# The short split tile of the first layer moves from last place to second place

## The chip, the cores and the metric

The kernel runs on one core of a Trainium2 chip. The metric is device time in microseconds (us) of one launch. The engines are TensorE (PE: matrix products and transposes; PEld: its weight loads), VectorE (DVE), ScalarE (ACT), GpSimd (POOL) and the queue engine SyncE (SP), which issues most of the DMAs. ScalarE issues some DMAs itself.

## The reference, cut to what matters

Three parts follow one another: a linear recurrence ("attention") over 4 sequences of 768 steps with 8 heads of 48, then two feed-forward layers on its 3072 x 384 output.

```python
# attention, for each step t
y[:, :, t] = einsum('bhd,bhde->bhe', rt, state + u[None] * kt (x) vt)
state      = wt[:, :, :, None] * state + kt (x) vt
# first layer, d_ff 2048
h = maximum(x @ w_in, 0);  x2 = (h * h) @ w_out
# second layer, d_ff 1536
out = ((x2 @ w_a) * (x2 @ w_b)) @ w_out2
```

## The kernel before, in words

**Units.** The recurrence is cut into chunks of 128 steps. One sequence's chunk is a *unit*; there are 24, ordered by chunk first, so that units 0 to 3 are chunk 0 of the four sequences, units 4 to 7 chunk 1, and so on. A unit passes through three functions: `prepare` (VectorE scans L197 and L202 and the scaled keys and receptances, GpSimd and ScalarE for the diagonal; it also issues the four loads of the unit after next, `load_unit(i + 2)`), `scores` (TensorE L239 and L243, VectorE L247) and `mix` (TensorE L261, L267 and L274, the new state L292 and L294, and six small SyncE copies, L287). A unit's result is 128 columns of the first layer's input. `split_x` (L306, L307) writes it as a rounded high part and a low rest into the input tile `xt[n]` of the first-layer tile it belongs to.

**First-layer tiles and stages.** The first layer runs over tiles of 2 or 4 units (256 or 512 columns). The list is `tiles`, L187. For each tile a stage of 16 steps runs. In step f, TensorE forms `hp` from `w_in[f]`, ScalarE and VectorE form relu squared (L463, L464), `split_g` splits it (L371, L372), and two steps later `x2_step` adds `w_out[f-2]` times it to three sums `acc`. At the end `store_acc` evicts the sums (L398) and stores them to DRAM. The tile in first place, units 0 and 1, is different: its products are plain fp32 products without a split (L417, L410; each counts as two matmuls in the trace). All others take three matmuls for each product, high by high, high by low and low by high (`mm3`, L311 to L313).

**What runs beside a stage.** While the stage of one tile runs, the units of the *next* tile are computed: `bursts` makes a plan that says after which step's `hp` the `scores` and the `mix` of a unit are issued; `BURSTS = (0, 2, 4, 6, 7, 9, 11, 13)` holds for four units. Before the change stage 0 (units 0 and 1) has units 2 to 5 beside it, stage 1 (units 2 to 5) has 6 to 9, stages 2, 3 and 4 have four units each, stage 5 (units 18 to 21) has the two units 22 and 23, and stage 6 (units 22 and 23, 256 columns) has none.

**Weights.** Weights arrive as 64-bit values. `decode` (L41 to L44, two ScalarE and two VectorE operations) turns one 128 x 384 block into fp32. The 32 blocks of the first layer are decoded in stage 0, two in a step. `split_w1` (L144, L145) splits them for `mm3`, from step 12 of stage 0 on and two in a step of stage 1. The 36 blocks of the second layer are loaded, decoded and stored back to DRAM as fp32 (`narrow_load`, `narrow_store`, called the narrow decodes here) from stage 2 on in the program's order; `load_w2` and `split_w2` (L167, L168) bring them in again during the last stage.

**Order.** Every engine works through its own queue in order. That order is not the program's: a planner, which schedules the instructions against its own estimate of the time, places work ahead where it finds an engine free and a buffer available, and otherwise takes the earlier part of the program first. Weight blocks share 36 buffers (`wp`), the loads of a unit have two (`ld`; `v` three), the input tiles two (`xp`), `A` two.

**Second layer.** Six tiles of 512 columns follow, 12 steps each, with TensorE alone near its limit.

Of the kernel before, what the change touches and what calls it, by code (L numbers as in the profile page):

```python
# [23 lines left out]
NU = len(units)  # L24
# [4 lines left out]
BURSTS = (0, 2, 4, 6, 7, 9, 11, 13)  # L29
# [18 lines left out]
@with_exitstack  # L48
def kernel(
    ctx: ExitStack,  # L50
    tc: tile.TileContext,
    krT: bass.AP,
    wT: bass.AP,
    krn: bass.AP,
    vn: bass.AP,
    u: bass.AP,
    w1: bass.AP,
    w2: bass.AP,
    w3: bass.AP,
    w4: bass.AP,  # L60
    w5: bass.AP,
    out: bass.AP,
):
    flags = ctx.enter_context(tc.tile_pool(name="flags", bufs=1))
    xs = ctx.enter_context(tc.tile_pool(name="xs", bufs=1, space=bass.MemoryType.DRAM)).tile([NT, DM], F32, name="xs")
    flag = chunked_path(tc, flags, krT, wT, krn, vn, u, w1, w2, w3, w4, w5, out)
    with tc.If(tc.nc.values_load(flag, min_val=0, max_val=1) > 0):
        stepwise_path(tc, xs, krT, wT, vn, u, w1, w2, w3, w4, w5, out)
# [3 lines left out]
def chunked_path(ctx, tc, flags, krT, wT, krn, vn, u, w1, w2, w3, w4, w5, out):  # L72
# [111 lines left out]
        loaded[i] = w, kr, v, nn  # L184

    xt = {}
    tiles = [(0, 1)] + [tuple(range(i, i + 4)) for i in range(2, NU - 2, 4)] + [(NU - 2, NU - 1)]  # L187
    x0 = {}
    unit = {}

# [62 lines left out]
    def mix(i):  # L253
# [22 lines left out]
        def post():  # L276
            if i > 1:
                x = at.tile([128, G, C], F32, tag="x", name="xf", bufs=2)
            else:
                if i == 0:  # L280
                    x0[0] = xp.tile([128, G, 2, C], F32, tag="x", name="x0")
                x = x0[0][:, :, i, :]
            for rows in ((slice(0, GP),) if c > 0 else (slice(0, D), slice(64, GP))):
                act.activation(out=x[rows], in_=ps[rows], func=AF.Copy)
            for p0 in (0, 64):
                for m in range(3):
                    sync.dma_start(out=x[p0 + 48:p0 + 64, m], in_=x[p0 + 16 * m:p0 + 16 * m + 16, 3])  # L287
            if c < NC - 1:
                src = pk[0:GP]
                if c > 0:  # L290
                    t = at.tile([GP, G, 2, D], F32, tag="kt", name="t")
                    dve.tensor_tensor(out=t, in0=src, in1=s[:, :, :, 0:D], op=ALU.add)  # L292
                    src = t
                dve.tensor_tensor(  # L294
                    out=s[:, :, :, 0:D], in0=src, in1=st["pe2"].to_broadcast([GP, G, 2, D]), op=ALU.mult
                )
            return (lambda: split_x(i, x)) if i > 1 else None
        return post

    def split_x(i, xf):  # L300
        n, o = (i + 2) // 4, (i + 2) % 4
        if n not in xt:
            xt[n] = xp.tile([128, 2, 3, T], F32R, tag="x", name="x")
        o = slice(o * C, (o + 1) * C)
        hi, lo = xt[n][:, 0, :, o], xt[n][:, 1, :, o]
        act.activation(out=hi, in_=xf[:, 0:3], func=AF.Copy)  # L306
        dve.tensor_tensor(out=lo, in0=xf[:, 0:3], in1=hi.bitcast(F32), op=ALU.subtract)  # L307
# [68 lines left out]
    def bursts(units_of, at_steps):  # L376

        return {f: (units_of[n // 2], n % 2) for n, f in enumerate(at_steps) if n // 2 < len(units_of)}
# [30 lines left out]
        for m in range(3):  # L409
            pe.matmul(out=acc[m], lhsT=w_out[f][:, m * 128:(m + 1) * 128], rhs=t, start=f == 0, stop=f == 15)  # L410

    plan = bursts(tiles[1], BURSTS)
    prepare(2)
    for f in range(16):
        hp = p_mm.tile([128, N], F32, tag="mm", name="hp")
# [6 lines left out]
        t = gg[f] = gp.tile([128, N], F32, tag="gh", name="g")  # L422
# [18 lines left out]
    for n in range(1, len(tiles)):  # L441
# [12 lines left out]
        plan = {} if last else bursts(tiles[n + 1], BURSTS)  # L454
        if not last:
            prepare(tiles[n + 1][0])
        for f in range(16):
# [4 lines left out]
            t = gp.tile([128, N], F32, tag="t", name="t", bufs=2)  # L462
# [265 lines left out]
```

## Time and profile before

| | us |
|---|---|
| median of 3 runs (1028.87 to 1030.48) | 1030.08 |
| profiled execution, its own time | 1029.76 |
| span from its first to its last instruction | 1028.1 |
| TensorE busy in it | 984.1 |
| VectorE busy | 540.5 |
| ScalarE busy | 448.3 |

The profiled execution is one launch; its span leaves 1.7 us outside the program's instructions. TensorE's matmuls overlap in the record (one of 512 columns shows some 0.39 us and the next begins after 0.23), so a busy TensorE is not TensorE at its pace; where pace matters, the starts of matmuls that follow each other are to be read. An edge between stages is taken where ScalarE begins the first eviction of a stage's sums (L398).

### The profile page before, as it was taken

The numbers are of one execution on the slowest core, as the hardware profiler recorded it, in microseconds if no ns is written. First come the engines' busy times: TensorE is split into PE (matmuls) and PEld (weight loads), VectorE is DVE, ScalarE is ACT, GpSimd is POOL, SyncE is SP. The second block draws the span as 40 slices with busy tenths as digits, with TensorE's granted clock in tenths as the row PEclk, the third lists the DMA queues.
The fourth block names the chain that finished last, engine by engine and source line by source line (L and its number), as shares of the span: only waits on it lengthen the run. The fifth ranks groups of instructions, "written<-read, shape, count | busy, mean of one in ns | idle before, by whom it ended". The sixth has DMA issues, their size and how long they took to land. (4 is left out here: it accounts for less than half of the span.)

```text
span 1028.1 us, 13834 instructions
## 1 busy us (share of the span) xinstructions
PE 984.1 (96%) x5250; PEld 834.4 (81%) x5250; DVE 540.5 (53%) x908; ACT 448.3 (44%) x930; POOL 72.7 (7%) x60
## 2 busy tenths in 40 slices
PE   3789999998999999999999999999999999999996
PEld 2577777777788888887889988888888888888885
DVE  8999999988856756644346622222222222222221
ACT  5788676777555444543336612222322312212211
POOL 4234201000100100000000000000000000000000
PEclk9999999999999999999999999999999999999998
DMA  9677237877422221201015400100100100000001
GB/s 274 218 254 244 67 95 254 258 257 244 146 83 64 77 67 54 65 21 54 23 46 155 132 1 2 61 1 21 41 1 1 41 1 16 27 1 32 0 1 34
DMA packets 47020, 88.15 MB, mean 86 GB/s; under 512 B 7008, under 2 KB 25568, under 8 KB 46944
## 3 DMA queue, kind: packets, MB, share of 16 engines
q1 hardware_dynamic: 40464, 77.74, 24.5%
q10 hardware_dynamic: 6480, 9.44, 2.6%
q8 instruction: 43, 0.70, 0.3%
q14 instruction: 33, 0.27, 0.1%
HBM read 69.46 MB, written 16.52 MB: 84 GB/s over the span
## 5 line engine op out<-in xcount | busy, mean ns | idle before, releaser
L536 DVE TENSOR_TENSOR t<-ap,t 128x512 f32<-128x512 f32 x72 | 49.8, 691 | 278.7 <-PE ap L313 278.7
L371 ACT ACTIVATE gh<-t 128x512 fp32r<-128x512 f32 (+1 forms) x168 | 102.4, 609 | 185.3 <-DVE t L536 127.0
L372 DVE TENSOR_TENSOR gl<-t,gh 128x512 fp32r<-128x512 f32 (+1 forms) x168 | 112.1, 667 | 74.7 <-ACT gh L371 74.4
L527 ACT ACTIVATE t<-bp 128x512 f32<-128x512 f32 x72 | 43.1, 598 | 160.4 <-PE bp L313 159.7
L311 PE MATMUL hp<-x,w 128*128 128x512 f32 (+1 forms) x288 | 109.3, 379 | 2.7 <-DVE t L464 2.7
L312 PE MATMUL acc<-gl,w 128*128 128x512 f32 (+1 forms) x288 | 108.2, 376 | 1.9 <-DVE gl L372 1.8
L313 PE MATMUL acc<-gh,w 128*128 128x512 f32 (+1 forms) x288 | 107.5, 374 | 0.0
L312 PE MATMUL hp<-x,w 128*128 128x512 f32 (+1 forms) x288 | 107.2, 372 | 0.0
L313 PE MATMUL hp<-x,w 128*128 128x512 f32 (+1 forms) x288 | 107.1, 372 | 0.0
L311 PE MATMUL acc<-gh,w 128*128 128x512 f32 (+1 forms) x288 | 102.6, 383 | 0.0
L464 DVE TENSOR_TENSOR t<-t,hp 128x512 f32<-128x512 f32 (+1 forms) x96 | 61.0, 635 | 74.0 <-ACT t L463 74.0
L518 PE MATMUL acc<-w,gh 128*128 128x384 f32 x288 | 96.8, 336 | 0.0
L519 PE MATMUL acc<-w,gh 128*128 128x384 f32 x288 | 96.7, 336 | 0.0
L520 PE MATMUL acc<-w,gl 128*128 128x384 f32 x288 | 95.1, 337 | 0.0
L463 ACT ACTIVATE t<-hp 128x512 f32<-128x512 f32 (+1 forms) x96 | 53.3, 555 | 83.2 <-PE hp L313 81.3
L313 PE MATMUL bp<-x,w 128*128 128x512 f32 x216 | 85.3, 395 | 0.0
L312 PE MATMUL bp<-x,w 128*128 128x512 f32 x216 | 85.1, 394 | 0.0
L312 PE MATMUL ap<-x,w 128*128 128x512 f32 x216 | 84.1, 390 | 0.0
L313 PE MATMUL ap<-x,w 128*128 128x512 f32 x216 | 84.1, 389 | 0.0
L311 PE MATMUL ap<-x,w 128*128 128x512 f32 x216 | 84.1, 389 | 0.0
L311 PE MATMUL bp<-x,w 128*128 128x512 f32 x216 | 83.8, 390 | 0.0
L311 PEld LDWEIGHTS hp<-x,w 128*128 128x128 f32 x288 | 54.2, 188 | 14.4 <-DVE t L464 4.3
(93 smaller groups left out, 1713.5 us busy)
## 6 DMA issues: line engine op xcount, KB each, us to landing
raw<-in_w SPq DMA_DIRECT2D x68, 384.0 KB, 4.7
lkr<-in_krT SPq DMA_DIRECT2D x24, 448.0 KB, 4.1
nn<-in_krn SPq DMA_DIRECT2D x24, 384.0 KB, 3.9
w2d<-f SPq DMA_DIRECT2D x36, 192.0 KB, 2.8
ws<-w2d SPq DMA_DIRECT2D x36, 192.0 KB, 2.5
lw<-in_wT SPq DMA_DIRECT2D x24, 226.2 KB, 3.4
vn<-in_vn SPq DMA_DIRECT2D x24, 192.0 KB, 2.8
out<-e ACTq DMA_DIRECT2D x24, 192.0 KB, 1.9
```

The lines of the kernel that those rows point to most:

```text
L311: pe.matmul(out=out, lhsT=wt[:, 0, sl], rhs=rhs_hi, start=first, stop=False)
L312: pe.matmul(out=out, lhsT=wt[:, 0, sl], rhs=rhs_lo, start=False, stop=False)
L313: pe.matmul(out=out, lhsT=wt[:, 1, sl], rhs=rhs_hi, start=False, stop=last)
L371: act.activation(out=gh, in_=t, func=AF.Copy)
L372: dve.tensor_tensor(out=gl, in0=t, in1=gh.bitcast(F32), op=ALU.subtract)
L463: act.activation(out=t, in_=hp, func=AF.Relu)
L464: dve.tensor_tensor(out=t, in0=t, in1=hp, op=ALU.mult)
L518: pe.matmul(out=acc[t], lhsT=ph[:, sl], rhs=w_o[f][:, 0, :], start=(f == 0), stop=False)
L519: pe.matmul(out=acc[t], lhsT=ph[:, sl], rhs=w_o[f][:, 1, :], start=False, stop=False)
L520: pe.matmul(out=acc[t], lhsT=pl[:, sl], rhs=w_o[f][:, 0, :], start=False, stop=(f == 11))
L527: act.activation(out=bs, in_=bp, func=AF.Copy)
L536: dve.tensor_tensor(out=bs, in0=ap, in1=bs, op=ALU.mult)
```

## The change

The first layer's tiles hold 2, 2, 4, 4, 4, 4 and 4 units in place of 2, 4, 4, 4, 4, 4 and 2. The tile in second place now has units 2 and 3, the next ones 4 to 7, 8 to 11, 12 to 15, 16 to 19 and 20 to 23. A table `place` tells `split_x` which tile and which quarter of it a unit has. Stage 0 has two units beside it, with their scores and mixes at steps 1, 5, 8 and 12; stages 1 to 5 have four units each, stage 6 has none and 512 columns.

```diff
     xt = {}
-    tiles = [(0, 1)] + [tuple(range(i, i + 4)) for i in range(2, NU - 2, 4)] + [(NU - 2, NU - 1)]
+    tiles = [(0, 1), (2, 3)] + [tuple(range(i, i + 4)) for i in range(4, NU, 4)]
+    place = {i: (n, o) for n, t in enumerate(tiles) for o, i in enumerate(t)}
     x0 = {}
...
     def split_x(i, xf):
-        n, o = (i + 2) // 4, (i + 2) % 4
+        n, o = place[i]
...
-    plan = bursts(tiles[1], BURSTS)
+    plan = bursts(tiles[1], (1, 5, 8, 12))
     prepare(2)
```

## Rows read from the trace of the kernel before

**Rows 1.** The page, busy time: us, share of the span, instructions of each engine.
```profile
PE 984.1 (96%) x5250; PEld 834.4 (81%) x5250; DVE 540.5 (53%) x908; ACT 448.3 (44%) x930; POOL 72.7 (7%) x60
```

**Rows 2.** Start and length of stage 0's first evictions on ScalarE.
```profile
121.84 0.65 ACT L398 ACTIVATE ev<-acc 128x256 f32<-128x256 f32 x2
```

**Rows 3.** Stages: length, busy of PE, PEld, DVE, ACT, POOL, clock, DMA share, GB/s.
```profile
0.00:43.54 43.54, 21.43 (x111) 17.06 (x111) 38.23 (x62) 25.75 (x61) 17.31 (x24) 1.00 0.76 236
43.54:121.84 78.30, 72.91 (x444) 60.32 (x444) 78.30 (x144) 61.02 (x145) 25.42 (x15) 1.00 0.66 210
121.84:210.63 88.79, 87.57 (x465) 68.72 (x464) 85.41 (x152) 66.29 (x141) 9.43 (x6) 1.00 0.61 194
210.63:298.09 87.46, 81.55 (x459) 64.88 (x458) 70.55 (x120) 54.86 (x120) 10.71 (x8) 1.00 0.58 187
298.09:382.78 84.69, 84.69 (x497) 69.41 (x496) 55.36 (x88) 40.34 (x88) 9.87 (x8) 1.00 0.24 73
382.78:465.21 82.43, 82.43 (x473) 67.14 (x472) 48.42 (x79) 39.48 (x86) 0.00 (x0) 1.00 0.16 48
465.21:536.98 71.77, 71.77 (x371) 59.22 (x370) 27.22 (x42) 24.65 (x44) 0.00 (x0) 1.00 0.12 35
536.98:582.09 45.11, 45.11 (x329) 42.64 (x328) 31.41 (x69) 30.40 (x71) 0.00 (x0) 1.00 0.55 162
```

**Rows 4.** The same stretches, VectorE's first scan of a unit (L197) alone.
```profile
0.00:43.54 43.54, 6.50 (x4) 1.00 0.76 236
43.54:121.84 78.30, 6.08 (x5) 1.00 0.66 210
121.84:210.63 88.79, 5.71 (x4) 1.00 0.61 194
```

**Rows 5.** Stage 1, VectorE's first decode operation (L42) alone.
```profile
121.84:210.63 88.79, 12.36 (x21) 1.00 0.61 194
```

**Rows 6.** Stage 1, VectorE's second decode operation (L44) alone.
```profile
121.84:210.63 88.79, 11.50 (x21) 1.00 0.61 194
```

**Rows 7.** VectorE groups of a step, shapes apart: count, busy us, mean ns, idle before.
```profile
L372 DVE TENSOR_TENSOR gl<-t,gh 128x512 fp32r<-128x512 f32 x152 | 105.3, 693 | 73.7 <-ACT gh L371 73.5
L464 DVE TENSOR_TENSOR t<-t,hp 128x512 f32<-128x512 f32 x80 | 54.3, 679 | 69.6 <-ACT t L463 69.6
L372 DVE TENSOR_TENSOR gl<-t,gh 128x256 fp32r<-128x256 f32 x16 | 6.7, 421 | 0.9 <-ACT gh L371 0.9
L464 DVE TENSOR_TENSOR t<-t,hp 128x256 f32<-128x256 f32 x16 | 6.7, 418 | 4.4 <-ACT t L463 4.4
```

**Rows 8.** First-layer weights on VectorE: ns min/median/max, first and last start us.
```profile
L44 DVE SCALAR_TENSOR_TENSOR wf<-raw,wf x32: 522/544/736, 30.0 to 110.3; 128x384 int32<-128x384 int32 x32
L145 DVE TENSOR_TENSOR w<-wf,w x32: 524/543/1368, 105.7 to 151.6; 128x384 fp32r<-128x384 f32 x32
```

**Rows 9.** TensorE in stages 4 and 6: start, length; nine matmuls between the two.
```profile
430.58 0.39 PE L311 MATMUL hp<-x,w 128*128 128x512 f32 x1
...
432.63 0.39 PE L311 MATMUL acc<-gh,w 128*128 128x512 f32 x1
...
556.59 0.28 PE L311 MATMUL hp<-x,w 128*128 128x256 f32 x1
...
557.67 0.28 PE L311 MATMUL acc<-gh,w 128*128 128x256 f32 x1
```

**Rows 10.** TensorE's parts of a unit: start, length.
```profile
123.16 0.55 PE L243 MATMUL pt<-ident,lkr 112*128 112x112 f32 x4
...
211.33 0.60 PE L261 MATMUL py<-lkr,s 112*112 112x128 f32 x4
211.87 1.08 PE L267 MATMUL py<-A,vn 128*48 128x128 f32 x16
212.88 1.02 PE L274 MATMUL pk<-vn,kt 128*112 128x96 f32 x8
...
436.80 1.16 PE L239 MATMUL ps<-lkr 48*128 48x128 f32 x16
```

## The prediction

> **What bounds the kernel now.** I read the busy times first: TensorE is busy for 96% of the span, VectorE for 53% [rows 1]. These are means over unlike stages, so I cut the span at the first eviction of each stage's sums (stage 0 ends at 121.84 us [rows 2]) and read the busy times stage by stage. The reader is to see two regimes [rows 3]. From 43.54 to 121.84 VectorE is busy for 78.30 of 78.30 us and in stage 1 for 85.41 of 88.79; TensorE's work has to wait for it there. From stage 3 on TensorE is busy all the time and VectorE for 59% and less: stages 3 and 4 (four units beside 512 columns) take 84.69 and 82.43 us, and 82.43 is what such a stage costs when nothing holds it up. Stage 2 lies between: 87.46 us, VectorE at 81%, with narrow decodes left over.
>
> The change alters no matmul. The same products run in the same shapes; a stage of 256 columns goes to the front and one of 512 to the end, and units 4 and 5, 8 and 9, 12 and 13, 16 and 17, 20 and 21 each run one stage later. So TensorE's own work is unchanged, and the time can change only by how long TensorE is held up, which is in the first 300 us. The sum is made by stages; what follows the first layer (from 582.09 us on) is taken as it is.
>
> **The change, part by part.**
>
> *Stages 0 and 1 together, by VectorE.* VectorE works for 38.23 + 78.30 + 85.41 = 201.9 us up to 210.63 us and idles 5.3 (before 43.54) and 3.4 us (stage 1) [rows 3]. Three things leave this stretch. Two units: stage 3 has 55.36 us of VectorE for four units and 16 steps; a step of 512 columns is 0.679 + 0.693 us [rows 7], so 16 are 22.0, and a unit is (55.36 - 22.0)/4 = 8.4 us; two are 16.8. The width: 16 x (0.679 + 0.693 - 0.418 - 0.421) = 8.5 us [rows 7]. The narrow decodes that run there now: 21, with 12.36 + 11.50 = 23.9 us [rows 5, 6], 1.14 us each. That leaves 201.9 - 16.8 - 8.5 - 23.9 = 152.7 us of work and with the old 8.7 us idle an end at 161.4.
>
> Two things correct it. First, work ahead: there are 9 first scans by 121.84 where stage 0 needs 6 (units 0 to 5), and 13 by 210.63 where 10 are needed [rows 4]. Three preparations therefore stand in the 201.9 us that the stretch didn't need. I put a preparation at two thirds of a unit, 5.6 us (an estimate), and take one fewer ahead, as the stretch is shorter: -5.6; the bounds are none fewer (0) and all three (-16.8). Second, some narrow decodes come back: they can't begin before the weight buffers come free, behind the last split at 151.6 [rows 8], which gave 21 in the 59 us up to 210.63; the splits end a little earlier after the change, some 15 us ahead of the new edge, so 5 of them: +5.7 us (bounds 0 and 8). Stage 1 would end at 161.4 - 5.6 + 5.7 = 161.5 us; bounds 152 (below) and 174 (the second rival). TensorE's side allows that: 288 matmuls of 256 columns at 1.08/9 = 0.120 us [rows 9] are 34.6 us. A unit is 0.55 + 2 x 0.60 + 1.08 + 1.02 + 1.16 = 5.0 us by its shown lengths [rows 10]; each carries a tail that the next covers (L267 shows 1.08 and is followed after 1.01), so I take 4.4, with 3.9 and 5.0 as ends. Four units make 17.6, stage 1's own work 52 us.
>
> ScalarE (61.02 of 78.30 and 66.29 of 88.79 us [rows 3]) loses its share of the same two units and of the width, so it stays under VectorE. On SyncE's queue the loads of units 6 and 7 (issued by `prepare` of 4 and 5) and twelve small copies leave stage 0; GpSimd has the two products of each unit with them. Both are far from full (GpSimd 25.42 of 78.30, DMA share 0.66 [rows 3]). I price that at nothing while VectorE sets the pace; if it doesn't, it helps stage 0. No wait is added; what changes is what stands in front of what on VectorE's queue.
>
> *Stages 2 and 3.* Both now have 512 columns and four units, as before. But 31 narrow decodes are left for them instead of 15. Stage 2 lost 87.46 - 82.43 = 5.0 us with 15, or 0.34 each; 31 cost 10.4, and stage 3's own loss of 2.3 stays. Together 2 x 82.43 + 10.4 + 2.3 = 177.5 us against 172.15. Bounds: 169 (decodes as pure filler with 0.1 each) and 190 (first rival's density and beyond). I take 0.34 because it is the only stage with both.
>
> *Stage 4:* 82.4 as before. *Stages 5 and 6:* 71.77 + 45.11 = 116.9 us now, with TensorE busy throughout. They gain two units (8.8) and 288 matmuls that go from 0.120 to (432.63 - 430.58)/9 = 0.228 us each [rows 9], 31.1 us: 156.8. The loads and splits of the second layer's weights that share stage 6 get more room, since VectorE's 31.41 us there grow by 8.5 and the stage by over 25; nothing is late next there. Bounds 155 and 159, by the unit's price and the edges.
>
> *Sum.* 161.5 + 177.5 + 82.4 + 156.8 = 578.2 us against 582.1: 3.9 less. The profiled execution took 1029.76 us (span 1028.1 and 1.7 around it), 0.3 under the median of 1030.08, so 1025.9; I say **1026 us**.
>
> *A rule that speaks against it.* TensorE was granted its full clock, 1.00 (2.4 GHz), in each of these stretches, also up to 43.54 where it is busy for 21.43 us [rows 3]. The Trainium skill, "TensorE: Matmul & The Clock Gate", section "What's actually happening", says that the engine falls back to 1.2 GHz after an idle spell, and the changed stage 1 leaves TensorE idle more often. By the rows the term is zero; by the rule it is the last rival.
>
> **The rivals.**
>
> *1. The decodes jam stage 2 (slower).* If the planner keeps three preparations ahead and the decodes go as early as they can, stage 1 ends at 161.4 + 5.7 = 167.1, and stage 2 has VectorE work of 55.36 + 31 x 1.14 = 90.7 us, more than the 82.4 of TensorE. At stage 1's density (85.41/88.79 = 96%) it takes 94.3. With 84.7, 82.4 and 156.8 the edge is at 585.3, +3.2: **1033**. It decides from a stage 2 over 94 us. For it: stage 2 already suffers with half as many decodes. Against: nothing needs them before the last stage, and the earlier part of the program goes first. At stage 2's own density of 81% it would be 112 us and 1051, the tail.
>
> *2. Stage 0 does not get shorter (slower).* The last of the 32 weight blocks is decoded at 110.3 us [rows 8] and the last steps need it; three preparations ahead say that VectorE had time beyond stage 0's own needs, so the stream of weights may set its end. Then stage 0 ends at 121.8 as now, stage 1 is TensorE's 52 us, ending at 174, decodes run in VectorE's spare time as today, stages 2 and 3 take 172.2: 174 + 172.2 + 82.4 + 156.8 = 585.4, +3.3: **1033**. Against: two units' loads fewer in the queue.
>
> *3. No work ahead (faster).* VectorE needs only 161.4 - 16.8 = 145 us, stage 0 ends near 100, and TensorE's 52 us end stage 1 at 152. With all 36 decodes after it (164.9 + 12.2 + 2.3 = 179.4), 82.4 and 156.8 the edge is at 570.6: **1018**. For it: the units are taken when they are needed. Against: in both edges of today three were ahead.
>
> *4. The clock falls in stage 1 (slower).* TensorE's 52 us at half the clock are 104: some 52 us more, **1078**. The granted 1.00 beside a half-idle TensorE speaks against it.
>
> **How the numbers follow.** Forecast 0.43, its own range 1021 to 1031; rival 1 0.18; rival 2 0.20; rival 3 0.17; rival 4 0.02. About 0.2% (2.1 us, 1028.0 to 1032.1) is what a measurement of this kernel tells from no change. Faster: 0.33 of the forecast and all of rival 3, 0.50. Within: 0.08 of the forecast, 0.05 each of rivals 1 and 2, 0.18. Slower: the rest, 0.32. The range of 1015 to 1037 takes in rivals 1 to 3 with a few us on either side and leaves out the tails.
>
> **What would show it.** In the changed profile: stage 0 ends between 95 and 112 us and stage 1 between 156 and 167, with VectorE busy for 95% and more up to there; fewer than 10 narrow decodes before that edge; stages 2 and 3 together some 177 us; stage 6 at some 74 us with TensorE busy all through; clock 1.00. A stage 0 over 118 is rival 2, a stage 2 over 94 with VectorE above 95% is rival 1, an edge of stage 1 at 152 or earlier rival 3. The prediction is wrong if stages 5 and 6 miss 156.8 by more than 3 us, since there I assumed that only TensorE counts.

## The result, and the profile after

The changed kernel takes 1040.4 us (median of 4 runs, 1039.29 to 1048.03), the kernel before 1029.88 in the same comparison: ratio 1.0122, 95% interval 1.0086 to 1.0158. The forecast was 1026, with a range from 1015 to 1037. The change makes the kernel slower, by 1.2%. The profiled span is 1037.6 us, 9.5 more than before.

First the page of the kernel after: the busy times, as in [rows 1], and the granted clock in 40 slices.

```profile
PE 990.3 (95%) x5250; PEld 842.1 (81%) x5250; DVE 536.7 (52%) x908; ACT 449.0 (43%) x930; POOL 78.0 (8%) x60
PEclk9899998999999999999999999999999999999999
```

The work is the same: 5250 matmuls, 908 VectorE instructions. The stages of the kernel after, cut as in [rows 3] (length, busy time of PE, PEld, DVE, ACT, POOL, clock, DMA share, GB/s); the edges are the first evictions of a stage's sums, and the last row is the second layer.

```profile
0.00:43.60 43.60, 19.68 (x111) 15.49 (x111) 37.05 (x62) 25.90 (x61) 19.13 (x24) 0.96 0.75 235
43.60:120.72 77.12, 70.71 (x411) 58.67 (x412) 77.12 (x143) 58.66 (x136) 22.07 (x13) 0.96 0.65 203
120.72:195.09 74.37, 68.49 (x512) 60.60 (x511) 69.52 (x138) 54.83 (x139) 16.50 (x8) 0.95 0.61 193
195.09:271.28 76.19, 72.74 (x356) 57.86 (x356) 59.68 (x106) 51.81 (x104) 5.02 (x4) 1.00 0.68 217
271.28:354.28 83.00, 83.00 (x482) 68.24 (x482) 56.21 (x90) 40.32 (x89) 9.87 (x8) 1.00 0.26 79
354.28:439.05 84.77, 84.77 (x498) 69.56 (x497) 53.93 (x88) 39.98 (x88) 5.46 (x4) 1.00 0.21 64
439.05:519.08 80.03, 80.03 (x451) 65.10 (x450) 38.25 (x63) 33.70 (x68) 0.00 (x0) 1.00 0.16 47
519.08:587.31 68.23, 68.23 (x302) 56.51 (x301) 38.37 (x66) 36.41 (x69) 0.00 (x0) 1.00 0.37 107
587.31:1037.60 450.29, 442.61 (x2138) 390.05 (x2136) 106.59 (x157) 107.41 (x183) 0.00 (x0) 1.00 0.06 18
```

The reader is to see three things. Stage 0 ends at 120.72, hardly before the old 121.84. Stage 1, with half the columns, still takes 74.37 us, and VectorE is busy for 69.52 of them. And the back as a whole is near the forecast: stages 4 to 6 and what follows them take 1037.6 - 354.28 = 683.3 us, where the forecast had 82.4 + 156.8 + 446.0 = 685.2 (its parts missed by more, see below). So the net error stands in the first 354 us: 354.3 measured, 161.5 + 177.5 = 339.0 forecast, 15.3 too little.

An edge of a stage is not an edge of TensorE's work: its first products of stage 2 start at 186.29 us, 9 us before stage 1 ends. The counts of TensorE instructions in brackets tell where two stages of the same number hold different work.

### The profile page after: what moved, and what is told of

It is laid out like the page before. It is cut to its first block, busy times and chain, and to the rows that moved or that the text cites. A ratio compares the mean times of both kernels' runs of the same rounds, so it can differ in the third digit from the quotient of the medians.

```text
span 1037.6 us, 13812 instructions
## 1 busy us (share of the span) xinstructions
PE 990.3 (95%) x5250; PEld 842.1 (81%) x5250; DVE 536.7 (52%) x908; ACT 449.0 (43%) x930; POOL 78.0 (8%) x60
```

## The experiments

All medians are compared with the kernel before in the same comparison (1029.7 to 1031.9 us there).

**Holding the units back.** Does stage 0 keep its length because units are prepared in it, or because of the stream of weights?

```diff
-    def prepare(i):
+    hold = [None]      # last step of the stage before, for units 4 to 11; then None
+    def prepare(i):
+        if hold[0] is None:
+            return prepare_now(i)
+        with tc.issue_after(hold[0]):
+            prepare_now(i)
...
```

> The changed kernel, all work kept, with VectorE's part of the preparation of units 4 to 7 queued behind the last step of stage 0, and of 8 to 11 behind the last step of stage 1. Theory A: work ahead on VectorE is what kept stage 0 at its old length, so it now ends at 98 to 108 us, and stage 1 ends at 172 to 185 us; 1025 to 1034 us. Theory B: the weights' stream sets the end of stage 0, so it still ends at 116 to 121 us, the units come too late and the kernel takes 1040 to 1055 us.

Measured: 1045.12 us, ratio 1.0154 (1.0126 to 1.0181). Stages 0, 1 and 2 of this kernel:

```profile
0.00:102.56 102.56, 74.11 (x386) 60.41 (x386) 91.65 (x173) 76.53 (x177) 20.38 (x25) 0.96 0.67 212
102.56:169.94 67.38, 61.20 (x478) 55.50 (x479) 60.31 (x116) 44.94 (x109) 10.03 (x8) 0.90 0.69 214
169.94:271.68 101.74, 91.57 (x508) 72.81 (x507) 95.95 (x160) 68.61 (x153) 24.34 (x16) 0.97 0.66 207
```

Stage 0 ends at 102.6, so the weights' stream does not set its end: the preparation of units on VectorE does. But stage 2 ends at 271.68 (271.28 without the hold): what was pushed back is paid there, and the total is no better, against the 1025 to 1034 that theory A expected.

**Without the narrow decodes on VectorE.** The two VectorE operations and one of the two ScalarE operations of each narrow decode are left out, so the second layer works on wrong weights.

```diff
-        sync.dma_start(out=w2d[n], in_=decode(nc, wr.tile(...), raw, near))
+        f = wr.tile([128, 384], F32, tag="ws", name="f")
+        high = raw.rearrange("p (n i) -> p n i", i=2)[:, :, 1]
+        act.activation(out=f, in_=high.bitcast(F32), func=AF.Copy, scale=0.05)
+        sync.dma_start(out=w2d[n], in_=f)
```

> The changed kernel with the 36 narrow decodes cut to one ScalarE copy each (no VectorE operation; the second layer then computes on wrong weights). Theory A, VectorE's queue sets the end of stage 1, because the planner still puts the decodes and the preparations of later units there: the 14 decodes that end before that edge leave it, some 15 us, so stage 1 ends near 180 us in place of 195 and the kernel takes 1022 to 1030 us. Theory C, TensorE's spells at half clock (17 us in the changed kernel's profile) make the loss: the time stays within 4 us of 1040. Theory B, the stream of first-layer weights sets it: stage 0 ends at 121 as before, which A also allows, and stage 1 still ends over 190.

> The kernel before with the same cut of the narrow decodes. Theory A: stages 1 and 2 lose less, stage 1 ends near 205 (210.6 before) and stage 2 takes 83 to 85 us (87.5), 1018 to 1024 us in all. So the changed order, without decodes, would be at most 8 us slower than the old one. Theory C: 1027 to 1031, no change, and the distance to the changed order stays at 10.

Measured: changed order 1030.16 us, ratio 0.9998 (0.9981 to 1.0015); old order 1025.02, 0.9944 (0.9922 to 0.9965). The changed order without them, stages 0 to 2:

```profile
0.00:120.76 120.76, 92.95 (x521) 76.56 (x522) 114.71 (x204) 84.59 (x198) 41.99 (x36) 0.99 0.69 215
120.76:174.53 53.77, 51.65 (x400) 46.39 (x400) 40.80 (x86) 37.82 (x99) 4.21 (x4) 1.00 0.59 198
174.53:260.59 86.06, 83.45 (x453) 66.52 (x452) 56.90 (x87) 49.59 (x108) 9.89 (x8) 1.00 0.73 240
```

Stage 1 falls from 74.37 to 53.77 us and VectorE in it from 69.52 to 40.80. A part of that is work of stage 2 that no longer runs there (TensorE has 400 instructions in place of 512). At the end of stage 2 the gain is 271.28 - 260.59 = 10.7 us. By the medians the decodes cost the changed order 10.2 us and the old one 5.0; 5 us between the orders remain.

**Putting the decodes later.** All of them kept, but none before the end of stage 1 (changed order) or of stage 2 (both orders), at one in 1.6 and 1.3 steps of the program.

```diff
-            elif (n - 2) * 16 + f >= narrow_n[0] * 1.6:
+            elif n > 2 and (n - 3) * 16 + f >= narrow_n[0] * 1.3:
...
+        with tc.issue_after(edge[0]):      # the last gl of stage 2 (or of stage 1, with 1.6)
             sync.dma_start(out=w2d[n], in_=decode(nc, wr.tile(...), raw, near))
```

> The changed kernel, all work kept, with VectorE's part of the narrow decodes queued behind the last step of stage 1 and spread over later steps. Theory A: stage 1 ends near 180 us, stages 2 and 3 pay for 36 decodes in place of 22 with 3 to 6 us, 1029 to 1035 us in all. Theory C: 1037 to 1041.

> The changed kernel, all work kept, with VectorE's part of the narrow decodes queued behind the last step of stage 2. Theory A2, the sum of VectorE's work up to the end of stage 2 sets that edge (271 to 272 us in the changed kernel and in both variants that only shifted work inside this stretch): the edge falls to 258 to 263 us as without the decodes, stages 3 and 4 have room for them at a cost of 0 to 3 us, and the kernel takes 1029 to 1034 us. Rival, the decodes cost TensorE the same wherever they run: 1038 to 1042.

> The kernel before with the same shift of the decodes behind stage 2. Theory A2: its end of stage 2 falls from 298 to 290 to 294 us, 1025 to 1029 us in all, faster than both kernels. Rival, the decodes cost the same wherever they run: 1029 to 1031.

Measured: changed order, behind stage 1, 1040.13 us, 1.0096 (1.0062 to 1.0130); behind stage 2, 1040.3, 1.0101 (1.0080 to 1.0121); old order, behind stage 2, 1035.15, 1.0047 (1.0027 to 1.0067). No gain anywhere, against the expectations. Stages 1 and 2 of the first, stages 2 and 3 of the second, and stage 3 of the third:

```profile
120.88:175.92 55.04, 52.91 (x405) 47.28 (x404) 44.98 (x92) 35.91 (x95) 4.63 (x4) 1.00 0.35 105
175.92:271.71 95.79, 90.67 (x486) 72.13 (x485) 83.75 (x146) 68.16 (x142) 10.77 (x8) 0.96 0.75 245
```

```profile
177.08:258.27 81.19, 81.19 (x450) 66.08 (x449) 55.85 (x90) 38.53 (x83) 9.28 (x8) 1.00 0.24 71
258.27:360.21 101.94, 93.73 (x522) 74.48 (x521) 87.68 (x154) 73.19 (x155) 15.21 (x8) 0.97 0.75 245
```

```profile
289.21:392.63 103.42, 95.03 (x527) 74.89 (x526) 87.08 (x154) 72.78 (x154) 17.89 (x8) 0.97 0.75 242
```

The stages freed of decodes become fast, and the one right behind the gate takes them all: VectorE's instructions in stage 3 rise from 90 to 154, 64 more for some 32 decodes of two each. Stage 3 takes 101.94 and 103.42 us where the kernels after and before need 83.00 and 84.69, although VectorE is busy for 86% and 84% of it only (30 to 40 more instructions of TensorE run in it, so not all of that is lost). So it was not VectorE's sum up to the end of stage 2 alone that mattered, as I had thought by then: the planner issues all decodes at once where it may.

**Spreading the decodes.** Each decode may start only behind the latest step's `gh` and `gl`, so that they come one by one in the program's order; all work is kept, in both orders.

```diff
+        with tc.issue_after(at_step[0]), tc.issue_after(at_step[1]):
             sync.dma_start(out=w2d[n], in_=decode(nc, wr.tile(...), raw, near))
...
+        at_step[:] = [a, d]      # split_g: the ScalarE copy gh and the VectorE subtraction gl
```

> The changed kernel, all work kept, with the VectorE and ScalarE operations of each narrow decode queued behind the step after which the program has it (one in 1.6 steps from stage 2 to stage 5), so that they can't gather. Theory A3, a decode costs because they gather in one stage: each stage from 2 to 5 loses 1 to 3 us more than its 4, 1030 to 1035 us in all. Rival, a decode has its price wherever it runs and however thin: 1038 to 1042.

> The kernel before, its decodes spread in the same way. Theory A3: 1024 to 1029 us, faster than both kernels. Rival, the same price everywhere: 1032 to 1036, as with all of them behind stage 2.

Measured: changed order 1029.5 us, 0.9991 (0.9978 to 1.0004); old order **1022.41, 0.9924 (0.9904 to 0.9945)**, a version that beats both kernels. Stages 1 to 3 of the changed order, spread:

```profile
119.86:174.90 55.04, 52.91 (x405) 47.28 (x404) 42.88 (x85) 32.21 (x89) 4.54 (x4) 1.00 0.31 93
174.90:256.36 81.46, 81.46 (x450) 66.12 (x449) 61.00 (x101) 45.28 (x98) 10.11 (x8) 1.00 0.41 121
256.36:341.64 85.28, 85.28 (x497) 69.69 (x496) 64.51 (x109) 50.24 (x108) 12.37 (x8) 1.00 0.46 144
```

and stages 1 and 2 of the old order, spread:

```profile
123.47:204.13 80.66, 79.56 (x427) 64.22 (x426) 62.76 (x107) 43.72 (x96) 8.28 (x6) 1.00 0.26 78
204.13:289.42 85.29, 85.29 (x499) 69.70 (x498) 64.38 (x106) 48.83 (x106) 11.29 (x8) 1.00 0.41 129
```

The stages that hold spread decodes (85.29, some ten in it) are within 0.6 us of one without (84.69 [rows 3]). Gathered as the planner likes, the same 36 decodes cost the changed order 1040.4 - 1029.5 = 10.9 us and the old one 1030.2 - 1022.4 = 7.8. Of the change's 10.5 us by medians, some 3 would thus be the gathering, and 7.1 stand between the two spread kernels. The first is not shown to be more than nothing, since the interval of the changed kernel (1.0086 to 1.0158) leaves 3.7 us of doubt in it. The second is: the runs of the two spread kernels don't overlap (1027.38 to 1031.80 and 1020.90 to 1024.55 us).

Part of the price may be ScalarE's, whose first decode operation waits for the load of the raw block: with gathered decodes such waits are long, in the kernel after between 120 and 272 us (engine, line waited for, us, times, longest):

```profile
ACT raw L41 <- DMA raw<-in_w: 23.2, 23, 2.8
```

The kernel before has 12.5 us of it between 120 and 298 us, the spread kernels none after 120. But the kernels without VectorE's decode work keep 15 and 22 us of such waits (for the raw block and for the store before it) and still run 10.2 and 5.0 us faster. How the price divides between VectorE's queue and ScalarE's waits stays open.

**The short tile elsewhere.** The old order with the short tile in fifth place.

```diff
-    tiles = [(0, 1)] + [tuple(range(i, i + 4)) for i in range(2, NU - 2, 4)] + [(NU - 2, NU - 1)]
+    tiles = [(0, 1)] + [tuple(range(i, i + 4)) for i in (2, 6, 10)] + [(14, 15), (16, 17, 18, 19), (20, 21, 22, 23)]
...
```

> The kernel before with the short split tile in fifth place (2, 4, 4, 4, 2, 4 and 4 units), so that its stage 4 has four units beside 256 columns, late enough for VectorE to have slack. Theory A2: VectorE needs some 34 us for the units and 13 for the steps there, TensorE 52, so nothing is lost: 1028 to 1032 us. Theory D, a short tile with four units beside it costs wherever it stands: 1036 to 1041.

Measured: 1030.36 us, 1.0006 (0.9994 to 1.0018). Its stage of 256 columns beside four units:

```profile
374.66:429.51 54.85, 54.85 (x509) 51.58 (x508) 44.59 (x90) 31.98 (x85) 4.44 (x4) 1.00 0.33 99
```

A short stage in this late place costs nothing, with VectorE at 81%. So a short stage with four units beside it is not dear by itself; it is dear in the early stretch.

**What the last 7 us are.** The subtraction for the low part of the first layer's 32 weight blocks (0.55 us each, 17.4 in all, in stages 0 and 1) is a piece of VectorE's work there that no unit needs. First it went to GpSimd:

```diff
-            dve.tensor_tensor(out=t[:, 1, :], in0=f, in1=t[:, 0, :].bitcast(F32), op=ALU.subtract)
+            pool.tensor_tensor(out=t[:, 1, :], in0=f, in1=t[:, 0, :].bitcast(F32), op=ALU.subtract)
```

> The changed kernel with the 32 subtractions that split the first layer's weights (L145, 17 us of VectorE in stages 0 and 1) on GpSimd. Theory A2: VectorE's sum up to the end of stage 2 falls by 17 us, that edge by 8 to 17, 1023 to 1032 us in all, unless GpSimd's own pace delays the splits. Theory C, the half clock: 1037 to 1041.

Measured: 1043.62 us, 1.0144 (1.0120 to 1.0169), no better than the changed kernel. Stage 0 grew from 120.7 to 123.9 us, and the splits ended later (ns min/median/max, first and last start):

```profile
L145 POOL TENSOR_TENSOR w<-wf,w x32: 988/1188/1929, 99.2 to 145.1; 128x384 fp32r<-128x384 f32 x32
```

GpSimd took 1.19 us for one where VectorE took 0.55, and began the last at 145.1 us in place of 137.8. VectorE's busy time up to the end of stage 2 fell by 4.5 us only (243.4 to 238.9) and not by the 16.5 of the subtractions, as others of its operations took longer. So the test hardly changed VectorE's sum and says little about it.

Then the subtraction was issued twice, in all four kernels:

```diff
-            dve.tensor_tensor(out=t[:, 1, :], in0=f, in1=..., op=ALU.subtract)
+            for _ in range(2):
+                dve.tensor_tensor(out=t[:, 1, :], in0=f, in1=..., op=ALU.subtract)
```

> The changed kernel with the 32 subtractions that split the first layer's weights (L145) done twice, 16 us of VectorE more in stages 0 and 1. If VectorE's sum sets the end of stage 2: that edge moves from 271 to 283 to 288 us and the kernel takes 1052 to 1057 us. If other waits set it: up to 5 us more.

> The kernel before with the same doubling. If its first stages hang on VectorE as much as those of the changed kernel: 1042 to 1046 us. If TensorE's longer stage 1 (65 us of matmuls in place of 35) covers a part of it, as the loss of the change would have it: 1034 to 1040 us.

> The changed order with spread decodes (1029.5 us) and the 32 weight splits of L145 done twice, some 16 us of VectorE more in stages 0 and 1. If VectorE is what is left of the loss in the short stage 1 (it is busy for 29 of the first 30 us there): stage 1 takes 8 to 15 us more, 1037 to 1045 us in all. If not: up to 4 us more.

> The old order with spread decodes (1022.4 us) and the same doubling. If TensorE's longer stage 1 covers VectorE there: 1 to 6 us more, 1023 to 1028. If VectorE counts the same under both orders: 1030 to 1038.

Measured: changed order 1047.98 us, 1.0165 (1.0145 to 1.0186); old order 1034.93, 1.0042 (1.0023 to 1.0061); spread, changed 1035.98, 1.0041 (1.0023 to 1.0060); spread, old 1027.91, 0.9970 (0.9954 to 0.9986). Against their own kernels the ratios rise by 0.0043, 0.0042, 0.0050 and 0.0046: 4 to 5 us each, none the full 17 and all alike (by medians the first pays 7.6). The two changed kernels fall between their two forecasts; the two old ones come out as forecast for a stage of TensorE's that covers a part. This alone would speak against VectorE as the cause of the 7 us. The profiles are less even. With spread decodes and the same work of TensorE done (within 3 instructions), the end of stage 2 moves by 7.9 us in the changed order (264.30 against 256.36) and by 3.1 in the old one (292.51 against 289.42). Stage 2 of the two spread kernels with the doubling:

```profile
193.85:264.30 70.45, 70.45 (x353) 56.92 (x352) 46.34 (x76) 38.99 (x81) 5.36 (x4) 1.00 0.36 111
209.43:292.51 83.08, 83.08 (x462) 67.07 (x461) 61.58 (x101) 47.91 (x104) 11.91 (x8) 1.00 0.40 123
```

That is the difference that a cover by the longer stage would make, but it is one execution of each, and the totals don't show it.

Last it was left out of both spread kernels, and the third product takes the high part again (the result is not the reference's):

```diff
...
-            dve.tensor_tensor(out=t[:, 1, :], in0=f, in1=t[:, 0, :].bitcast(F32), op=ALU.subtract)
+            dst[n] = HighTwice(t)      # index 0 for both parts
```

> The changed order with the narrow decodes spread one by one, and without VectorE's 32 subtractions for the low part of the first layer's weights (the third product takes the high part again, so the result is not the reference's): some 32 x 0.54 = 17.4 us of VectorE less in stages 0 and 1, TensorE's work unchanged. The spread kernels stand 7 us apart (1029.5 against 1022.4). Theory D (in the changed order VectorE's backlog at the end of stage 1 is what the other order covers with a longer stage): the changed order gains more by the relief than the old one, the gap falls to 0 to 3 us, this kernel at 1015 to 1021. Theory E (the gap doesn't come from VectorE's sum): both gain the same, some 4 to 6 us as doubling cost 5, this kernel at 1023 to 1026, and the gap stays at 5 to 9 us.

> The order before the change with the narrow decodes spread, and without the same 32 subtractions of VectorE (third product with the high part again). Both theories: 4 to 6 us less than 1022.4, so 1016 to 1019, by the 5 us that doubling the same instructions cost. Theory D: the changed order comes within 3 us of it. Theory E: the changed order stays 5 to 9 us above it.

Measured: changed order 1022.21 us, 0.9923 (0.9895 to 0.9951); old order 1021.59, 0.9924 (0.9896 to 0.9952). The gap is closed, as theory D has it (their runs overlap, 1019.44 to 1025.61 and 1020.21 to 1024.20), though both times lie some 1 and 3 us above what was expected. The rest of stage 0 and stages 1 and 2 of the changed order:

```profile
43.70:118.66 74.96, 70.00 (x393) 58.17 (x394) 71.52 (x130) 62.61 (x150) 24.09 (x13) 0.94 0.65 204
118.66:164.60 45.94, 45.45 (x385) 42.52 (x384) 29.15 (x61) 24.80 (x66) 3.13 (x3) 1.00 0.33 104
164.60:249.79 85.19, 85.19 (x490) 69.42 (x489) 63.93 (x106) 47.81 (x105) 12.05 (x10) 1.00 0.41 124
```

and of the old order:

```profile
43.70:121.97 78.27, 72.35 (x440) 59.85 (x438) 78.13 (x142) 67.62 (x162) 25.30 (x15) 0.98 0.67 212
121.97:201.17 79.20, 79.20 (x431) 64.63 (x430) 48.43 (x76) 36.82 (x81) 6.69 (x7) 1.00 0.26 77
201.17:286.45 85.28, 85.28 (x499) 69.70 (x498) 64.42 (x106) 48.62 (x105) 10.90 (x8) 1.00 0.41 128
```

17 us of VectorE less gain 7.3 us in the changed order and 0.8 in the old one. In the changed order stage 1 goes from 55.04 to 45.94 us, a part of which is 20 instructions of TensorE that now run in stage 2; at the end of stage 2, with as much of TensorE's work done, it is 6.6 us (256.36 to 249.79). In the old order stage 1 hardly moves (80.66 to 79.20), and the 3.0 us that it is ahead at the end of stage 2 don't reach the end. In the traces of the two spread kernels TensorE waits next to nothing for a split (0.4 us, once, in the old order), so what the cut relieves is VectorE's time and not a direct wait for the low parts. The 7 us between the spread kernels are thus the price of VectorE's splits. The reading that the old order's 512-column stage covers them fits this. That 17 us more cost both alike is no contradiction, for cover that is just used up gives no gain below and a price above; that is an argument, and why the changed order pays only some 5 of the 17 was not tested.

## Why the prediction was wrong

Stage 1 ended at 195.09 us, 33.6 after the 161.5 of the sum and outside its bounds of 152 to 174.

**The step that failed first: two units leave stages 0 and 1.** The sum took 16.8 us out of VectorE's work for them and 5.6 more for one preparation fewer ahead. The first scans (their line is now L198) in the same stretches as [rows 4], in the kernel after:

```profile
0.00:43.60 43.60, 5.77 (x4) 0.96 0.75 235
43.60:120.72 77.12, 6.09 (x5) 0.96 0.65 203
120.72:195.09 74.37, 4.87 (x4) 0.95 0.61 193
```

9 by the end of stage 0 and 13 by the end of stage 1, the same counts as before. The stages need fewer units now, and the planner prepares as many as before. With 4 and 8 needed there, 9 and 13 mean five ahead at both edges instead of three. Not only the preparations ran ahead. TensorE's product of `mix` (L268, 16 instructions a unit) in the same stretches:

```profile
0.00:43.60 43.60, 5.82 (x34) 3.68 (x34) 0.96 0.75 235
43.60:120.72 77.12, 5.80 (x72) 4.01 (x72) 0.96 0.65 203
120.72:195.09 74.37, 6.24 (x70) 4.02 (x70) 0.95 0.61 193
```

176 instructions, 11 whole units by the end of stage 1, where 8 are needed; before there were 161, 10 units, and all 10 were needed. That is what the bound "none fewer" should have held and did not: it still let the two units leave.

The kernel with the units held back shows what this step alone is worth. There 9 units are prepared and 8 mixed by the end of stage 1, and that end comes at 169.94 us, inside the bounds. But then stage 2 takes 101.74 us and not the 82.43 + 10.4 = 92.8 of the sum, with 21 narrow decodes and VectorE busy for 95.95 us of it, and stages 0 to 3 come to 356.4 in place of 339.0. So the forecast fails with the units gone from the stretch, too, there by the price of what comes after it.

**Second: 5 decodes come back.** VectorE's two decode operations (L42, L44) in stage 1 of the kernel after, and the last splits and all narrow decodes (ns min/median/max, first and last start):

```profile
120.72:195.09 74.37, 7.86 (x14) 0.95 0.61 193
120.72:195.09 74.37, 6.54 (x12) 0.95 0.61 193
L145 DVE TENSOR_TENSOR w<-wf,w x32: 527/550/558, 102.5 to 137.8; 128x384 fp32r<-128x384 f32 x32
L44 DVE SCALAR_TENSOR_TENSOR f<-raw,f x36: 518/551/585, 147.9 to 260.5; 128x384 int32<-128x384 int32 x36
```

12 to 14, not 5. The splits end at 137.8, 14 us earlier than in [rows 8] and 57 us ahead of the edge, where the sum had 15. The decodes use the time behind them, ahead of steps that TensorE waits for. A stretch of VectorE's queue there (start, length) shows how two decode operations lie, with work of units, between the `t` of a step (175.42) and its `gl` (178.93):

```profile
175.42 0.41 DVE L465 TENSOR_TENSOR t<-t,hp 128x256 f32<-128x256 f32 x1
...
176.09 0.74 DVE L248 COPY_PREDICATED A<-mask,ps 128x512 f32<-128x512 int32 x1
...
176.79 0.68 DVE L209 TENSOR_TENSOR lkr<-lkr,fq 112x512 f32<-112x512 f32 x1
177.39 0.68 DVE L210 TENSOR_TENSOR lw<-fq 112x512 f32<-112x512 f32 x1
177.99 0.55 DVE L44 SCALAR_TENSOR_TENSOR f<-raw,f 128x384 int32<-128x384 int32 x1
178.46 0.55 DVE L42 SCALAR_TENSOR_TENSOR f<-raw 128x384 int32<-128x384 int32 x1
178.93 0.42 DVE L373 TENSOR_TENSOR gl<-t,gh 128x256 fp32r<-128x256 f32 x1
```

With the two counts taken from the trace the same sum comes out: 201.9 - 8.5 (the width) - 7 x 1.14 (7 to 9 decodes fewer) = 185.4 us of VectorE, measured 37.05 + 77.12 + 69.52 = 183.7, plus some 11 idle: 196, measured 195.1. So adding up VectorE's work held and the counts put into it did not: 16.8 + 5.6 + 8 = 30.4 us too little, and some 3 us of idle time more than the old 8.7.

**0.34 us for a decode in stages 2 and 3.** The number was never put to the test. Stages 2 and 3 came to 159.2 us, 18.3 under the 177.5, because work done ahead in stage 1 was missing there (TensorE has 512 instructions in stage 1 of the kernel after, 400 in the one without narrow decodes). That gave back about half of the 33.6 us that stage 1's end was late, an offset that the sum had not counted and that was luck. The price of a decode depends on how many come at once. With some 32 gathered in stage 3 that stage takes 101.94 us against 85.28 spread, both in the changed order, and the whole kernel 1040.3 - 1029.5 = 10.8 us more. Spread, they cost a stage some 0.6 us.

**The ledger.** Up to the end of stage 2 the change gains 298.09 - 271.28 = 26.8 us. From there to the end of stage 6 it costs 582.09 - 298.09 = 284.0 against 587.31 - 271.28 = 316.0, 32.0 us, by the stage that is now 512 columns wide; what follows takes 450.3 against 446.0, 4.3 more, as 26 matmuls of the second layer ran before that edge and 50 before the change. 32.0 + 4.3 - 26.8 = 9.5. The move is a bargain only if the front gains what the back pays, and it did not.

**The rivals.** Rival 2's sign came true (stage 0 over 118), but not its mechanism: the weights' stream does not set the end, since holding units back brings it to 102.6. Rival 1 had the planner's mechanism, decodes as early as they can go and work ahead kept; but it put the jam into stage 2, where VectorE is busy for 78%, and it came in stage 1, at 93% (with the units held back it does come in stage 2). Rival 3 is refuted by the scans. Rival 4: TensorE was granted half its clock (0.50) in four spells, 39.9 to 46.7, 53.6 to 57.0, 162.8 to 166.2 and 176.4 to 179.8 us, 17 us in all. They explain little of the time. Stage 0 ends at 120.72 with a clock of 0.96, at 120.76 without the decodes with 0.99 and at 119.86 in the spread kernel, which has the full clock up to the end of stage 2 and is still 7 us behind its twin. In the two spells of stage 1 TensorE was busy throughout (3.40 of 3.40 us each), so there the half clock can have cost up to 3.4 us (an estimate: half of their 6.8 us); no run separates that from the gathered decodes. The forecast's own sentence "by the rows the term is zero" was wrong as to the clock and nearly right as to the time. The Trainium skill, "TensorE: Matmul & The Clock Gate", section "What's actually happening", has the engine fall to 1.2 GHz after idling. This trace agrees in so far as each fall came in or soon after a wait of TensorE for VectorE, of 4.09, 1.07, 0.63 and 0.82 us, but idle spells of 2.45 and 1.43 us that ended at 29.82 and 32.85 us brought none.

**The back.** Stages 5 and 6 were put at 156.8 us and took 80.03 + 68.23 = 148.3; the prediction named a miss of over 3 us there as a sign against it, and the sign came. Stage 4 took 2.4 more than its 82.4, and what follows the first layer 4.3 more, so the sum to the end missed by only 1.9. Most of this is work on another side of an edge: of the 8.5, 5.5 are the 24 matmuls of the second layer (24 x 0.228) that now run after it.

## What to carry to other kernels

Where a planner or a queue may work ahead, work that a stage no longer needs may not leave it, as here: count the instructions that will *run* there, not those that the program puts there, and price the change once with none of them leaving. Filler work behind a gate was issued all at once here when the gate opened; tie each piece to a step of the main work, and it may be nearly free: that alone made the old order 0.76% faster (1.0 - 0.9924). A short stage belongs where the engine that feeds it has room: in fifth place it cost nothing, in second place 1.2%.

## What the runs showed of the hardware that was not expected

The profile of the kernel after has 17 us of spells at half the granted clock (0.50, 1.2 GHz) up to 180 us, and that of the kernel before has none there. They are not a mark of the change: over its runs the kernel before has a mean clock of 0.984 to 0.998, and the kernel after 0.990 to 0.995. In stage 0, where TensorE waits for VectorE, their price is some 1 us at most. In the changed order that stage ends at 120.72, 120.76 and 120.88 us with a mean clock of 0.96, 0.99 and 0.94 (the last with the decodes behind stage 1), and at 119.86 with 1.00.

The same VectorE operation did not take the same time in all kernels. With the 32 subtractions on GpSimd, VectorE's 16 `gl` of 256 columns took 521 ns each on average and its 14 operations of L207 up to the end of stage 2 took 944, where the kernel after has 414 and 757. What lengthened them was not looked into.
